# A root chain in two parts, and the four sums of y shared anew between VectorE and GpSimd

## The chip, the cores and the metric

The kernel runs on one core of a Trainium2 chip. A core has a matmul engine (TensorE, PE in the profile; its weight loads are PEld), VectorE (DVE), ScalarE (ACT), GpSimd (POOL) and SyncE (SP), each with its own instruction queue that runs in order, and 16 DMA engines. SBUF is the on-chip working memory, PSUM the memory that matmuls write, in eight banks. The metric is the device time in microseconds (us), the median of several runs.

## The reference

Two blocks follow each other on x of shape (8, 4224, 192), all in float32.

```python
# block 1: causal convolution, 7 taps, one softmaxed tap vector per head (8 heads of 24 channels)
w = softmax(weight, axis=-1)
y[b, s, h, g] = sum_k w[h, k] * x_pad[b, s + k, h, g]
# block 2: layer norm without shift, two matmuls, residual
mu, var = mean(y), mean((y - mu) ** 2)            # over the 192 channels
xn = (y - mu) / sqrt(var + 1e-6) * g_ln
out = y + relu(xn @ w_ch1) @ w_ch2                # 192 -> 768 -> 192
```

The mean and g_ln are folded into w_ch1 once, at the start, and the factor 1/sqrt(var + 1e-6), here rstd, is positive, so it passes through the relu: the kernel multiplies the un-normalised y and scales each row of the product with rstd at the end.

## The kernel before

**Tiles.** The rows are cut into 18 groups. Groups 0 to 2 are small (6, 8 and 10 rows on each of 128 partitions); groups 3 to 17 hold 16 rows on each partition. Groups 3 to 17 are the "mixed" ones, and this text is about them.

**Two stages per group.** `up_mixed(g)` makes the hidden layer (line L521 of the profile), `down_fast(g)` the second matmul (L789). Both use a Winograd form of Strassen's scheme: both operands are cut into four quarters, and seven products of quarters take the place of eight. Each stage so has seven products, 504 matmul instructions for a whole group. What this saves on TensorE is paid in sums on the other engines: sums of y's quarters (`sums_of_y`, L575 to L579), of the weights' quarters (made once), and of the results' quarters (closings and half sums).

**Sums of y.** With quarters a11, a12, a21, a22 of the transposed y, the products need s1 = a21 + a22, s2 = s1 - a11, s3 = a21 - a11 (the sign is taken up in the weights) and s4 = a12 - s2. Before the change GpSimd makes s3 and s2 (L575, L576), and VectorE makes s4 and s1 after the moments (L578, L579). The order of products in the up stage is a11, a12, s2, s3, s1, a22, s4.

**The up stage in two passes.** Pass one is for one third of the hidden columns (PAIR..FC), pass two for the rest. The result's quarters c11, c12, c21, c22 lie in SBUF. ScalarE evicts a product from PSUM (`evict`, L616); a later product that is to be added to a quarter is "closed" (`close`): ScalarE evicts it to a spare place and GpSimd issues a DMA that adds it (`add_by_dma`, L583). In pass one the spare places are parts of pass two's own quarters: c12's for the closings of c11 and c22, c22's for the closing of c21. So ScalarE may not evict into pass two's c22 before the DMA that adds c21 has read its source. In pass two the spare places are two other tiles (parts_cs, parts_tb). In the last group the closings are VectorE's (L622), without DMA.

**The down stage.** Four products, then on VectorE nine half sums over the hidden quarters (L756, three for each of three sums), then three products that need them. Between products ScalarE evicts (L795) and works off a list `work`: a relu of a quarter of the hidden layer (L629), scales of the group before (L869), and the first two taps of the convolution of group g + 2 (L383, L394). The second tap is added to y by two DMAs that GpSimd issues (L397), in order, behind ScalarE's part of them. At the stage's end VectorE takes the moments (L439) of group g + 1 and the sums of its y are made.

**The root.** rstd of two groups is made at once on GpSimd by `root(g)`, after the down stage of each odd group from 3 on (groups 3 and 4 together, 5 and 6, and so on to 15 and 16), and of group 17 alone after that of group 16. It is a chain of 19 small instructions of 128x32 (L457 to L470): seven for the variance and the first guess, then three Newton steps of four. GpSimd's queue before the up stage of an even group is therefore: the two adds of the second tap, s3, s2, the chain, a memset in the input tile of group g + 2 (L160), and then the three closing adds of pass one.

**Order.** No planner reorders anything: each engine runs its instructions in the order in which the program text emits them, and waits on semaphores for what others made. Generators (`yield`, `next`) are used to emit a function's instructions in parts at given places of another.

Of the kernel before, what the change touches and what calls it, by code (L numbers as in the profile page):

```python
# [11 lines left out]
ALU = mybir.AluOpType  # L12
# [4 lines left out]
def kernel(  # L17
# [29 lines left out]
    nc = tc.nc  # L47
# [22 lines left out]
    groups = [(0, 0, 6), (None, 0, LEFT), (0, 6, J - 6), (0, J, J)]  # L70
# [352 lines left out]
    sums = {}  # L423
# [14 lines left out]
        for j in range(j1, n if j2 is None else j2):  # L438
            nc.vector.bn_stats(out=sums[g][:, j, :], in_=y[g][:, j, :])  # L439

    def root(g):
        both = [k for k in (g, g + 1) if k < NG and chain_of(k) == g]
        n = sum(groups[k][2] for k in both)
        st = sums[g]
        dt = spool.tile([P, 2 * J], F32, tag="d", name=f"d{g}")
        vt = spool.tile([P, 2 * J], F32, tag="v", name=f"v{g}")
        rt = spool.tile([P, 2 * J], F32, tag="r", name=f"r{g}")
        d, v, r = dt[:, 0:n], vt[:, 0:n], rt[:, 0:n]

        def affine(dst, src, scale, bias):  # L450
            nc.gpsimd.tensor_scalar(
                out=dst, in0=src, scalar1=scale, scalar2=bias, op0=ALU.mult, op1=ALU.add
            )

        nc.gpsimd.tensor_tensor(d, st[:, 0:n, 1], st[:, 0:n, 4], op=ALU.subtract)  # L457
        nc.gpsimd.tensor_tensor(v, st[:, 0:n, 2], st[:, 0:n, 5], op=ALU.add)
        nc.gpsimd.tensor_tensor(d, d, d, op=ALU.mult)
        affine(v, v, 1.0 / D, 1e-6)  # L460
        affine(d, d, 0.25, 0.0)
        nc.gpsimd.tensor_tensor(v, v, d, op=ALU.add)


        affine(r.bitcast(I32), v.bitcast(I32), -0.5, float(0x5F3759DF))
        for _ in range(3):
            nc.gpsimd.tensor_tensor(d, r, r, op=ALU.mult)  # L467
            nc.gpsimd.tensor_tensor(d, d, v, op=ALU.mult)
            affine(d, d, -0.5, 1.5)
            nc.gpsimd.tensor_tensor(r, r, d, op=ALU.mult)  # L470
        for k in both:
            rstd[k] = rt[:, (k - g) * groups[g][2] :]

    def store_y(g, queue=nc.sync):
        n = groups[g][2]
# [92 lines left out]
    def sums_of_y(g, engine):  # L568

        room = upool.tile([P, 3 * HJ * CH * C], F32, tag="ys", name=f"ysums{g}")  # L570
        room = room.rearrange("p (v j c t) -> p v j c t", v=3, c=CH, t=width(g))
        s2, s3, s4 = [room[:, v] for v in range(3)]
        a11, a12, a21, a22 = quarters_of_y(g)
        ysums[g] = a21, s2, s3, s4
        engine.tensor_tensor(s3, a21, a11, op=ALU.subtract)  # L575
        engine.tensor_tensor(s2, s3, a22, op=ALU.add)  # L576
        yield
        nc.vector.tensor_tensor(s4, a12, s2, op=ALU.subtract)  # L578
        nc.vector.tensor_tensor(a21, a21, a22, op=ALU.add)  # L579
        yield  # L580

    def add_by_dma(dst, src):
        nc.gpsimd.dma_start(out=dst, in_=src, accum_op=ALU.add)  # L583

    def up_mixed(g, ahead):


        W = HJ * C
# [60 lines left out]
        p.evict(X, p.c11)  # L649
        p.product(Y, a12, p.b21)  # L650
        p.close(p.c11, Y, two.c12[:, 0:1])
        p.product(X, s2, p.t[0], False, False)
        p.evict(X, p.c21)
        p.product(Y, s3, p.t[1], True, False)
        p.evict(Y, p.c22)
        p.product(X, s1, p.b12, False, False)
        p.close(p.c22, X, two.c12[:, 1:2])
        p.product(Y, a22, p.t[2], False)
        p.close(p.c21, Y, two.c22[:, 0:1])
        p.product(X, s4, p.b22, False)  # L660
# [28 lines left out]
        p.close(p.c22, Y, rooms[1][:, 0:PAIR])  # L689
        p.product(X, a22, p.t[2], False)  # L690
        p.relu(p.c11)
        lower_sum(g, (PAIR,))
        p.close(p.c21, X)
        p.product(Y, s4, p.b22, False)
# [7 lines left out]
        taps_of_next(5, 6, heads=(H // 2, H))  # L702
        taps_of_next(6, K)

        work = [lambda: one.relu(one.c22)]

        def scale_one(j):
            scale(g - 1, j, j + 1)
            if j == 7:
# [1 line left out]
            elif j == done - 1:  # L711
                add_to_out(g - 1, 8, done)

        if not last:
            work += [lambda j=j: scale_one(j) for j in range(2, done)]
        half = [lambda i=i: two.relu(two.c22[:, i : i + 1]) for i in range(PAIR)]
        return work[0:9] + half + work[9:]

# [53 lines left out]
    def down_fast(g, work):  # L772
        n = fast[g]
        t = width(g)
        w = n * T
        a = of_products(g)
        flat = cpool.tile([P, NC, NFAST * C], F32, tag="cs", name=f"cs{g}")[:, :, 0 : n * C]
        order = "p c (h j t) -> p c h j t" if t == C else "p c (j h t) -> p c h j t"
        cs = flat.rearrange(order, h=2, t=t)
        free = a[:, 1, 0].rearrange("p f q j t -> p (f q) j t")  # L780
        parts = [free[:, 0:CH], free[:, CH : 2 * CH]]
        banks = [take_bank() for c in range(CH) for i in range(2)]

        def product(bank, left, right, to, first, behind=0):
            for c in range(CH):
                dst = banks[2 * c + bank]
                for f in (PAIR, *range(PAIR)):
                    for q in range(NQ):
                        nc.tensor.matmul(  # L789
                            dst[C * q : C * q + C, 0:w], right[:, f, C * c : C * c + C],  # L790
                            left[:, f, q], start=(first and f == PAIR), stop=(f == PAIR - 1),
                            skip_group_check=True,
                        )
                if to is not None:
                    nc.scalar.copy(  # L795
                        to[:, c], dst[:, 0:w].rearrange("p (j t) -> p j t", t=t)
                    )
                for one in work[:behind]:
                    one()
                del work[:behind]  # L800

        b = quarters_of_w2()
        c11, c21 = cs[:, 0:CH, 0], cs[:, 0:CH, 1]
        c12, c22 = cs[:, CH:NC, 0], cs[:, CH:NC, 1]
        if g + 2 < NG:
            work += [
                lambda tap=tap, h=h: tap(g + 2, heads=(h, h + 1))
                for tap in (first_tap, second_tap) for h in range(H)
            ]
        product(0, a[:, 0, 0], b[0], c11, True, 3)  # L810
        product(1, a[:, 1, 0], w2sums[:, 2], c22, True, 2)
        product(1, a[:, 1, 1], w2sums[:, 3], c21, False, 2)
        product(1, a[:, 0, 1], b[2], None, True, 3)
        if g + 1 < NG:
            transpose(g + 1)
        half_sum(g, (1, 1), (1, 1), (1, 0), ALU.add)
        half_sum(g, (0, 0), (1, 1), (0, 0), ALU.add)
        half_sum(g, (0, 1), (0, 1), (1, 1), ALU.subtract)
        for c in range(CH):
            nc.vector.tensor_tensor(  # L820
                c11[:, c], c11[:, c], banks[2 * c + 1][:, 0:w].rearrange("p (j t) -> p j t", t=t),
                op=ALU.add,
            )
        product(0, a[:, 1, 1], w2sums[:, 1], parts[0], False, 2)
        product(0, a[:, 0, 0], w2sums[:, 0], parts[1], False, 2)
        for one in work:
            one()
        product(0, a[:, 0, 1], b[3], c12, False)
        if g + 1 < NG:
            moments(g + 1)  # L830
            sums = sums_of_y(g + 1, nc.gpsimd)
            next(sums)
            next(sums)
        else:
            finish_fast(g, 0, flat, cs, parts)
        return flat, cs, parts
# [92 lines left out]
    split_words(*words_2)  # L929
    join_words(w2flat, *words_2)  # L930
    store_y(0)
    results = None

    def ahead(g):

# [6 lines left out]
    for g in range(NG):  # L942
        mixed, last = g in MIXED, g + 1 == NG
        if g + 2 < NG:
            load_x(g + 2)
        if mixed:
            work = up_mixed(g, ahead(g))
        else:
            up(g)
        if not fast[g]:  # L950

            conv(g + 1)
            transpose(g + 1)
            if g < 2:
                store_y(g + 1)
                moments(g)
            first_tap(g + 2)
            if g == 2:

                second_tap(g + 2)  # L960
                store_y(g + 1, nc.gpsimd)
            down(g)
            park(g)
            if g == 1:
                finish(0)
                root(0)
                sums_of_quarters([w2sums[:, v] for v in range(4)], *quarters_of_w2())
                moments(2)
                root(2)
                finish(1)  # L970
            elif g == 2:
                b11, b12, b21, b22 = quarters_of_w1()
                sums_of_quarters([b12] + [w1sums[:, v] for v in range(3)], b11, b12, b21, b22)
                later = sums_of_y(3, nc.vector)
                next(later)
                next(later)
                finish(2)
                moments(3)
            continue
        if g + 2 < NG:  # L980
            store_y(g + 1)
        results = down_fast(g, work)
        if last:
            finish_fast(g, 1, *results)
            add_and_store(g, slice(0, fast[g]))
            down(g)
            finish(g)
        else:
            if g % 2:
                root(g)  # L990
            if g + 2 == NG:
                root(g + 1)


# [28 lines left out]
```

## Time and profile before

| what | value |
|---|---|
| time, median of 3 (lowest to highest) | 979.66 us (979.08 to 981.59) |
| span of the profiled execution | 978.0 us, mean granted TensorE clock 0.996 |
| TensorE, VectorE, ScalarE, GpSimd busy | 955.8, 902.2, 680.8, 261.6 us |
| one half sum, L756 | mean 1.24 us for 135 |
| GpSimd's sums of y, L575 and L576 | 2.50 and 1.95 us on average, 14 each |
| first instruction of the chain, L457, 128x32 | 2.66 us |
| taps of the convolution on VectorE, L408 | 734 instructions, 367 us |
| closing adds room<-room, 512 KB each | 42, median 5.9 us from issue to landing |

The page of a run gives busy times of each engine, then the costliest groups of instructions by line of the program, with what the engine waited for before them. The trace behind it answers for any stretch of time: the order of instructions on each engine, and for each idle time what ended it ("0.86 <-DMA room<-room" means 0.86 us idle until that DMA had landed). A matmul counts as busy until its modelled end, so how long a fixed set of matmuls takes from first start to next stage's first start says more than the busy time. Idle time of an engine off the bound costs nothing.

### The profile page before, as it was taken

The page shows a single profiled execution, that of the slowest core. Times are in us where ns is not written, and L with a number is a line of the kernel's source. Part 1 is how long each engine was busy: PE and PEld are TensorE (multiplying, and loading weights), DVE is VectorE, ACT ScalarE, POOL GpSimd, SP SyncE. Part 2 cuts the span into 40 slices and gives each one's busy share as a digit, 9 for nine tenths or more (in the row PEclk, how much of TensorE's full clock was granted, in tenths as well). Part 3 has the DMA queues.
Part 4 walks back from the last instruction along what each step waited for, and adds up shares of the span by engine and source line. Part 5 has one row for each costly group of instructions (what it writes and reads, how often), then busy time and mean ns, then how long its engine had stood idle before and what let it go on. Part 6 is the DMA issues. An engine that isn't in the chain of part 4 may idle for free.

```text
span 978.0 us, 38335 instructions
## 1 busy us (share of the span) xinstructions
PE 955.8 (98%) x17274; PEld 724.3 (74%) x17274; DVE 902.2 (92%) x1491; ACT 680.8 (70%) x1098; POOL 261.6 (27%) x383
## 2 busy tenths in 40 slices
PE   7999999999999999999999999999999999998997
PEld 6886586676858677786958678786867768695787
DVE  6999999989999999989999899989989899999757
ACT  5625678487787959677796968678695868775351
POOL 2005311612125131512116131532117121342200
PEclk9999999999999999999999999999999999999999
DMA  8343887479787786879687795978777796856031
GB/s 179 116 137 118 174 210 214 105 144 281 143 239 155 212 188 141 231 153 267 137 240 153 185 231 115 269 146 237 160 203 167 145 275 132 192 114 109 2 68 67
DMA packets 26386, 165.15 MB, mean 169 GB/s; under 512 B 3567, under 2 KB 4463, under 8 KB 18542
## 3 DMA queue, kind: packets, MB, share of 16 engines
q0 software_dynamic: 19120, 99.36, 52.0%
q1 hardware_dynamic: 6798, 63.34, 17.6%
q8 instruction: 135, 2.21, 0.9%
q14 instruction: 29, 0.24, 0.1%
q10 hardware_dynamic: 304, 0.00, 0.0%
HBM read 38.95 MB, written 50.33 MB: 91 GB/s over the span
## 4 chain that ended last, share of the span: by engine, by line
PE 72%; DVE 10%; DMA 6%; POOL 5%; ACT 4%; issue 2%; SPq 0%; ACTq 0%; DVEq 0%; POOLq 0%
PE ps L521 36%; PE ps L789 30%; DVE room L756 6%; PE ps L736 6%; DMA room<-room 5%; DVE st L439 2%; POOL d L457 1%; ACT room L616 1%; DMA xg<-in_x_dram 1%; ACT ot L869 1%; ACT room L629 1%; POOL d L467 1%; POOL r L470 1%; POOL room L583 1%; ACT cs L795 1%
## 5 line engine op out<-in xcount | busy, mean ns | idle before, releaser
L408 DVE SCALAR_TENSOR_TENSOR y<-xg,taps,y 128x384 f32<-128x384 f32 (+3 forms) x734 | 367.0, 577 | 1.2 <-ACT y L383 0.6
L789 PE MATMUL ps<-room,w2sums 128*32 128x256 f32 (+1 forms) x4320 | 238.5, 377 | 4.5 <-DVE room L756 3.1
L521 PE MATMUL ps<-yt,w 32*128 32x256 f32 (+2 forms) x4104 | 238.6, 379 | 0.0
L616 ACT COPY room<-ps 128x1024 f32<-128x1024 f32 (+1 forms) x132 | 172.0, 1303 | 83.1 <-PE ps L521 78.5
L521 PEld LDWEIGHTS ps<-yt,w 32*128 32x128 f32 x4104 | 203.6, 185 | 27.5 <-issue 7.0
L789 PEld LDWEIGHTS ps<-room,w2sums 128*32 128x32 f32 x4320 | 142.5, 110 | 95.6 <-DVE room L756 6.7
L789 PE MATMUL ps<-room,w 128*32 128x256 f32 (+1 forms) x3240 | 182.4, 378 | 2.5 <-DVE room L756 2.4
L756 DVE TENSOR_TENSOR room<-room 128x1024 f32<-128x1024 f32 (+1 forms) x135 | 157.8, 1241 | 7.6 <-PE ps L789 7.6
L789 PEld LDWEIGHTS ps<-room,w 128*32 128x32 f32 x3240 | 107.4, 111 | 69.7 <-DVE room L622 5.2
L521 PE MATMUL ps<-ysums,w1sums 32*128 32x256 f32 x2160 | 123.9, 377 | 0.0
L521 PEld LDWEIGHTS ps<-ysums,w1sums 32*128 32x128 f32 x2160 | 110.6, 185 | 9.6 <-issue 1.8
L795 ACT COPY cs<-ps 128x256 f32<-128x256 f32 (+1 forms) x180 | 66.3, 371 | 47.0 <-PE ps L789 47.0
L629 ACT ACTIVATE room<-room 128x1024 f32<-128x1024 f32 (+1 forms) x75 | 90.8, 1235 | 9.9 <-DMA room<-parts_cs 9.5
L869 ACT ACTIVATE ot<-ot,r 128x192 f32<-128x192 f32 x232 | 93.8, 463 | 0.0
L876 POOL DMA_DIRECT2D out_dram<-ot x40 | 34.4, 1091 | 204.5 <-ACT ot L869 126.1
L622 DVE TENSOR_TENSOR room<-room,ps 128x2048 f32<-128x2048 f32 (+1 forms) x20 | 42.5, 2128 | 45.5 <-PE ps L521 45.3
L383 ACT ACTIVATE y<-xg,taps 128x384 f32<-128x384 f32 (+3 forms) x141 | 72.7, 609 | 8.2 <-DVE st L439 6.9
L439 DVE BATCH_NORM_STATS2 st<-y 128x6 f32<-128x192 f32 x264 | 70.1, 341 | 0.0
L795 ACT COPY room<-ps 128x256 f32<-128x256 f32 (+1 forms) x90 | 33.7, 374 | 49.8 <-PE ps L789 46.9
L521 PE MATMUL ps<-yt,w1sums 32*128 32x256 f32 x1080 | 65.0, 379 | 2.8 <-ACT room L616 2.7
L521 PE MATMUL ps<-ysums,w 32*128 32x256 f32 x1080 | 64.8, 378 | 0.0
L394 ACT ACTIVATE tb<-xg,taps 128x384 f32<-128x384 f32 x112 | 62.0, 637 | 0.0
(103 smaller groups left out, 894.9 us busy)
## 6 DMA issues: line engine op xcount, KB each, us to landing
xg<-in_x_dram SPq DMA_DIRECT2D x15, 2112.0 KB, 17.7
out_dram<-ot POOLq DMA_DIRECT2D x29, 768.0 KB, 8.7
y<-tb POOLq DMA_DIRECT2D x28, 768.0 KB, 10.7
room<-room POOLq DMA_DIRECT2D x42, 512.0 KB, 5.9
out_dram<-y SPq DMA_DIRECT2D x13, 1536.0 KB, 9.9
room<-parts_cs POOLq DMA_DIRECT2D x14, 1024.0 KB, 8.5
room<-parts_tb POOLq DMA_DIRECT2D x14, 1024.0 KB, 7.5
xg<-in_x_dram SPq DMA_DIRECT2D x1, 1536.0 KB, 8.0
```

The source lines that it names most:

```text
L383: nc.scalar.mul(y[g][:, 0:n, cs], xg[g][:, 0:n, cs], taps[:, h, 0:1])
L394: nc.scalar.mul(tb[g][:, 0:n, cs], xg[g][:, 1 : 1 + n, cs], taps[:, h, 1:2])
L408: nc.vector.scalar_tensor_tensor(out=y[g][:, 0:n, cs], in0=t[:, k : k + n, cs], scalar=taps[:, h, k : k + 1], in1=y[g][:, 0:n, cs], op0=AL ...
L439: nc.vector.bn_stats(out=sums[g][:, j, :], in_=y[g][:, j, :])
L521: nc.tensor.matmul(banks[:, q, i * w : i * w + w], right[rows, c, P * i : P * i + P], left[rows, :, c, :], start=(first and c == 0 and i = ...
L616: nc.scalar.activation(dst, src, AF.Relu) if relu else nc.scalar.copy(dst, src)
L629: nc.scalar.activation(c, c, AF.Relu)
L736: nc.tensor.matmul(bank[C * q : C * q + C, 0:w], w2[:, f, C * c : C * c + C], left, start=(f == 0), stop=(f == NF - 1),)
L756: nc.vector.tensor_tensor(a[:, *dst, f], a[:, *left, f], a[:, *right, f], op=op)
L789: nc.tensor.matmul(dst[C * q : C * q + C, 0:w], right[:, f, C * c : C * c + C], left[:, f, q], start=(first and f == PAIR), stop=(f == PAI ...
L795: nc.scalar.copy(to[:, c], dst[:, 0:w].rearrange("p (j t) -> p j t", t=t))
L869: nc.scalar.mul(ots[g][:, j, :], ots[g][:, j, :], rstd[g][:, j : j + 1])
```

## The change

There are four edits.

1. `root` becomes a generator of two parts. Part one is the variance, the first guess and the first two multiplications of Newton's first step (nine instructions), part two the other ten. `up_mixed` emits part one behind the closing of c11 in pass one, part two behind the closing of c22, so that the closing adds don't all stand behind the whole chain. The roots of the first groups are emitted whole, as before.
2. `sums_of_y`: VectorE makes s1 and s2 first, ahead of the moments; GpSimd makes s3 and s4. s1, s2 and s3 lie in the tile ysums, s4 takes the place of a21.
3. When GpSimd makes its two, VectorE first writes one element of s3 with a memset. GpSimd's write of s3 must then wait for that memset, which stands behind VectorE's half sums and its own two sums.
4. In the last group the relus of c22 (both passes) are emitted in the up stage ahead of the last lower sums, and no longer from the list `work` in the down stage.

```diff
-    def root(g):
+    def root(g, whole=False):
...
-        for _ in range(3):
+        for k in both:
+            rstd[k] = rt[:, (k - g) * groups[g][2] :]
+        for step in range(3):
             nc.gpsimd.tensor_tensor(d, r, r, op=ALU.mult)
             nc.gpsimd.tensor_tensor(d, d, v, op=ALU.mult)
+            if step == 0 and not whole:
+                yield
             affine(d, d, -0.5, 1.5)
             nc.gpsimd.tensor_tensor(r, r, d, op=ALU.mult)
-        for k in both:
-            rstd[k] = rt[:, (k - g) * groups[g][2] :]
+        yield
...
-        s2, s3, s4 = [room[:, v] for v in range(3)]
+        s1, s2, s3 = [room[:, v] for v in range(3)]
         a11, a12, a21, a22 = quarters_of_y(g)
-        ysums[g] = a21, s2, s3, s4
+        ysums[g] = s1, s2, s3, a21
+        nc.vector.tensor_tensor(s1, a21, a22, op=ALU.add)
+        nc.vector.tensor_tensor(s2, s1, a11, op=ALU.subtract)
+        if engine is not nc.vector:
+
+            nc.vector.memset(s3[:, 0:1, 0:1, 0:1], 0.0)
         engine.tensor_tensor(s3, a21, a11, op=ALU.subtract)
-        engine.tensor_tensor(s2, s3, a22, op=ALU.add)
-        yield
-        nc.vector.tensor_tensor(s4, a12, s2, op=ALU.subtract)
-        nc.vector.tensor_tensor(a21, a21, a22, op=ALU.add)
-        yield
+        engine.tensor_tensor(a21, a12, s2, op=ALU.subtract)
...
         p.close(p.c11, Y, two.c12[:, 0:1])
+        next(pending, None)
         p.product(X, s2, p.t[0], False, False)
...
         p.close(p.c22, X, two.c12[:, 1:2])
+        next(pending, None)
         p.product(Y, a22, p.t[2], False)
         p.close(p.c21, Y, two.c22[:, 0:1])
...
         p.relu(p.c11)
+        if last:
+            one.relu(one.c22)
+            p.relu(p.c22)
         lower_sum(g, (PAIR,))
...
-        work = [lambda: one.relu(one.c22)]
...
-        if not last:
-            work += [lambda j=j: scale_one(j) for j in range(2, done)]
+        if last:
+            return []
+        work = [lambda: one.relu(one.c22)]
+        work += [lambda j=j: scale_one(j) for j in range(2, done)]
...
         if g + 1 < NG:
+            sums_of_y(g + 1, nc.gpsimd)
             moments(g + 1)
-            sums = sums_of_y(g + 1, nc.gpsimd)
-            next(sums)
-            next(sums)
...
-            work = up_mixed(g, ahead(g))
+            work = up_mixed(g, ahead(g), pending)
+            pending = iter(())
...
-            if g % 2:
-                root(g)
-            if g + 2 == NG:
-                root(g + 1)
+            if g % 2 or g + 2 == NG:
+                pending = root(g + 1 - g % 2)
```

More of the change, by code (lines that the diff above doesn't have):

```diff
@@ L571, in sums_of_y, with up_mixed @@
         room = room.rearrange("p (v j c t) -> p v j c t", v=3, c=CH, t=width(g))
-        s2, s3, s4 = [room[:, v] for v in range(3)]
+        s1, s2, s3 = [room[:, v] for v in range(3)]
         a11, a12, a21, a22 = quarters_of_y(g)
-        ysums[g] = a21, s2, s3, s4
-        engine.tensor_tensor(s3, a21, a11, op=ALU.subtract)
-        engine.tensor_tensor(s2, s3, a22, op=ALU.add)
-        yield
-        nc.vector.tensor_tensor(s4, a12, s2, op=ALU.subtract)
-        nc.vector.tensor_tensor(a21, a21, a22, op=ALU.add)
-        yield
+        ysums[g] = s1, s2, s3, a21
[3 more added lines that the diff above has]
+            nc.vector.memset(s3[:, 0:1, 0:1, 0:1], 0.0)
+        engine.tensor_tensor(s3, a21, a11, op=ALU.subtract)
+        engine.tensor_tensor(a21, a12, s2, op=ALU.subtract)
     def add_by_dma(dst, src):
         nc.gpsimd.dma_start(out=dst, in_=src, accum_op=ALU.add)
-    def up_mixed(g, ahead):
+    def up_mixed(g, ahead, pending):
         W = HJ * C
@@ L931 @@
     store_y(0)
-    results = None
+    results, pending = None, iter(())
     def ahead(g):
@@ L965 @@
                 finish(0)
-                root(0)
+                next(root(0, True))
                 sums_of_quarters([w2sums[:, v] for v in range(4)], *quarters_of_w2())
                 moments(2)
-                root(2)
+                next(root(2, True))
                 finish(1)
@@ L973 @@
                 sums_of_quarters([b12] + [w1sums[:, v] for v in range(3)], b11, b12, b21, b22)
-                later = sums_of_y(3, nc.vector)
-                next(later)
-                next(later)
+                sums_of_y(3, nc.vector)
                 finish(2)
```

## The prediction

> **What bounds the kernel now.** First the page's busy times, then the matmuls in order of time, cut into stages.
>
> ```profile
> PE 955.8 (98%) x17274; PEld 724.3 (74%) x17274; DVE 902.2 (92%) x1491; ACT 680.8 (70%) x1098; POOL 261.6 (27%) x383
> ```
>
> TensorE is the bound, so an edit can only earn what TensorE loses against its own best stage. I cut the timeline where its line changes from L521 (up) to L789 (down) and asked for busy time by stretch. Columns: stretch, length, busy time per engine, granted clock, DMA share, GB/s. The down stages of groups 3, 4 and 16:
>
> ```profile
> 150.72:182.45 31.73, 29.32 (x508) 17.39 (x504) 31.70 (x44) 20.86 (x45) 8.67 (x7) 0.95 0.82 221
> 211.19:238.63 27.44, 27.44 (x508) 16.16 (x504) 27.40 (x44) 22.72 (x51) 7.21 (x6) 1.00 0.87 238
> 881.70:914.12 32.42, 29.34 (x509) 16.77 (x505) 32.26 (x45) 15.15 (x36) 8.21 (x5) 0.95 0.41 71
> ```
>
> The same 504 matmuls take 27.44 us in a good stage, 4.29 more in group 3, 4.98 more in group 16. About half is idle, the rest a granted clock of 0.95 after the wait. The timeline of VectorE and GpSimd there, beside the same nine half sums of group 7:
>
> ```profile
> 389.88 10.26 DVE L756 TENSOR_TENSOR room<-room 128x1024 f32<-128x1024 f32 x9
> ...
> 893.88 13.52 DVE L756 TENSOR_TENSOR room<-room 128x1024 f32<-128x1024 f32 x9
> ...
> 894.14 2.63 POOL L575 TENSOR_TENSOR ysums<-yt 128x768 f32<-128x768 f32 x1
> 896.84 2.66 POOL L576 TENSOR_TENSOR ysums<-ysums,yt 128x768 f32<-128x768 f32 x1
> ```
>
> GpSimd's sums of y ran inside the half sums, 3.3 us longer, and the product needing the first ones waited 3.08 us (the waits of PE name DVE room L756). In group 3 both sums also fall inside (13.84 us). Elsewhere GpSimd is held until the half sums are nearly over by the two adds of L397 (398.86 in group 7); group 16 has none, in group 3 they come earlier.
>
> Next the up stages. Groups 8, 14 and 16, behind which a root chain runs, and group 9, which has none:
>
> ```profile
> 405.27:434.00 28.73, 28.24 (x508) 25.25 (x504) 25.60 (x42) 20.27 (x17) 13.53 (x25) 1.00 0.73 146
> 741.36:770.63 29.27, 28.23 (x508) 25.25 (x504) 25.47 (x41) 20.27 (x17) 13.75 (x25) 1.00 0.72 145
> 853.74:881.70 27.96, 27.96 (x509) 25.36 (x505) 25.48 (x41) 20.17 (x17) 13.07 (x24) 1.00 0.64 128
> 461.44:489.40 27.96, 27.96 (x509) 25.36 (x505) 25.56 (x42) 20.27 (x17) 4.36 (x5) 1.00 0.74 148
> ```
>
> All stages without a chain take 27.96. The seven with one (groups 4, 6 to 16 in twos) take 28.74, 28.05, 28.73, 28.94, 28.31, 29.27 and 27.96: 4.28 us too long together. The timeline of group 8 says why:
>
> ```profile
> 416.10 2.42 POOL L583 DMA_DIRECT2D room<-room  x3
> ...
> 426.69 1.87 ACT L616 COPY room<-ps 128x2048 f32<-128x2048 f32 x1 [0.86 <-DMA room<-room]
> ...
> 428.61 2.47 PEld L521 LDWEIGHTS ps<-yt,w1sums 32*128 32x128 f32 x48 [0.89 <-ACT room L616]
> ```
>
> The chain fills GpSimd from 405.39 to 415.16, then a 1.05 us memset; only then do the three closing adds go out, in a burst. The third (c21's) lands 9.3 us after its issue at 417.26; ScalarE may not overwrite its source before, and TensorE stands behind ScalarE.
>
> Last, group 17's down stage:
>
> ```profile
> 945.90 2.95 ACT L629 ACTIVATE room<-room 128x1024 f32<-128x1024 f32 x3
> ...
> 949.51 2.89 PE L789 MATMUL ps<-room,w2sums 128*32 128x176 f32 x72 [0.94 <-ACT cs L795]
> ```
>
> Three relus hold up the evictions that free the banks: 144 matmuls take 6.51 us (945.71 to 952.22), the next 144 only 5.37 (954.91 to 960.28). Loss 1.14 us.
>
> **What the skill says.** The Trainium skill, "SBUF — State Buffer", section "Who interferes with whom": a VectorE instruction with two SBUF inputs and a GpSimd instruction that reads SBUF exclude each other for a whole instruction; one with a single SBUF input contends with nothing. The trace agrees: 13.5 against 10.3 us for L756; but L576 beside the one-input moments L439 takes 1.84 us and the 16 moments keep their 4.25. "GPSIMD Engine Reference", "Performance versus the Vector engine", puts an fp32 add at 1.96 times VectorE's; here 1.84 (L576) against 0.94 (L578), the same. "DMA: Bandwidth & Descriptors", "Anatomy of one DMA", says waits and dispatch happen on the issuing sequencer, so an add queued behind arithmetic on GpSimd leaves late; group 8's adds left 10.8 us into the stage, group 9's first 5.0.
>
> **The change part by part.** Times are those of group 8's boundary.
>
> *Sums of y.* VectorE keeps two sums of this size (0.93 and 0.95) and GpSimd two (1.84 each). New is a one-element memset (59 ns, L216) per boundary, and it gates GpSimd: its sums start behind all half sums, L820 and VectorE's two sums, at about 403.0 in group 8. Neither can meet L756 any more. They run beside the moments (402.9 to 407.2, one input), so I take 1.84 each: end 406.75, just ahead of the two-input L842. Needed: s2 at 408.07, made by VectorE at 402.8; s3 at about 409.4, ready 404.9; s4 at 413.52, ready 406.75. No wait. VectorE's 0.06 us is hidden by its 2.2 to 2.7 us of idle ahead of L622. Gain: groups 3 and 16 fall to 27.44, **4.29 + 4.98 = 9.27 us**. With half sums of 1.14 us, the third, sixth and ninth are ready at 897.3, 900.7, 904.1 in group 16, and products of 3.9 us start at 897.4, 901.3, 905.1.
>
> *The root in two parts.* GpSimd's queue becomes: sums, memset of xg (about 408), c11's add, part one (nine instructions), c22's add, part two (ten), c21's add. Most other groups' first add leaves 4.25 us into the stage, here 409.5, busy 0.88. Part one from 410.4: beside one-input transposes an instruction and its gap cost 0.31 us (411.19 to 413.12), the first waits for L842 until 410.9; end 413.9. Source c22 is ready at 413.43, so its add leaves about 414.0, free 414.9. Part two lies beside the two-input taps L408, where four instructions took 1.98 us (413.12 to 415.1): 10 x 0.5 = 5, end 420.0. c21's add therefore leaves at 420.0, *later* than now (417.26), but alone: lone adds landed in 5.3 and 4.4 us in group 9, so about 425.0. ScalarE gets there at 425.83. Bounds on the landing: 4.2 (shortest of all) to 6.9 us (group 9's third, behind another), that is 424.2 to 426.9; the upper end is today's wait again. I take 5.0: the waits go, 0.1 us per group remains; **3.6 of 4.28 us**. Queued behind part two is only c21's add: pass two's parts_cs add leaves at 422.58 now, with GpSimd idle 4.1 us before it. The scale waiting for rstd is at 422.18 on ScalarE, 2.2 us after part two. Group 17's root is off the path: its closings are VectorE's.
>
> *Relus of the last group.* They move into ScalarE's 4.26 us of idle before 942.86: from 938.6, 1.06 us, then 1.9 us once VectorE's close ends at 939.87: end about 941.8. Gain **1.14 us**.
>
> *Keeping rstd earlier in the text, running the first roots whole, group 3's sums in another order:* the same instructions, nothing.
>
> Sum: 9.27 + 3.6 + 1.14 = 14.0; 979.66 - 14.0 = **965.7 us**.
>
> **Rivals.**
> A. *The root's split earns nothing*: part two ahead of c21's add replaces the burst's delay by its own. For it: the add leaves 2.7 us later and my margin is 0.8 us. Against: it lands alone. Time: 979.66 - 10.4 = 969.3.
> B. *The new order of sums costs a little at each boundary*: GpSimd meets L842, or VectorE finishes later. For it: the end of s4 lies 0.4 us ahead of L842. Against: six microseconds of slack for s4, two on VectorE. At 0.2 us for 14 boundaries: 965.7 + 2.8 = 968.5.
> C. *Slower*: if c21's add still needs 9 us, it lands at 429.0, ScalarE waits 3.2 us instead of 0.86, seven times 2.3 = 16 us instead of a gain: 979.66 - 10.4 + 16 = 985. Against: no first add of a burst took over 5.5 us in group 8, and none is ahead of it.
>
> **How the numbers follow.** Forecast 0.70, A 0.15, B 0.09, C 0.06. The range reaches down to all of 14.7 us plus the 1.2 us by which three down stages behind late chains (groups 6, 12, 14) exceed 27.44: 963.8, and a run's scatter: 963.3. Up: A and a little of C, 971.5. Faster means under 976.7: the first three cases, 0.94; the same 0.01; slower 0.05.
>
> **What would show it.** Right: down stages of groups 3 and 16 near 27.4 with nine half sums in 10.3 us and GpSimd's sums behind them at 1.84; stages with a chain at 28.0 to 28.1, no ScalarE wait on DMA room<-room, single adds landing in about 5; group 17's first 144 w2sums matmuls in 5.4. Wrong: c21's add leaving after 421 or landing after 426; scales waiting for GpSimd; TensorE waiting for s3 or s4.

## The result, and the profile after

The changed kernel takes **964.04 us** (median of 4 runs, 962.95 to 965.15) against 979.39 us for the kernel before, measured beside it (979.08 to 981.59): ratio 0.9839, 95% interval 0.9819 to 0.9858, or 15.4 us less. Forecast were 965.7 us, range 963.3 to 971.5.

The page's first line of busy times, now for a span of 962.8 us:

```profile
PE 950.3 (99%) x17274; PEld 717.0 (74%) x17274; DVE 897.2 (93%) x1505; ACT 680.9 (71%) x1097; POOL 249.4 (26%) x383
```

Busy time by stretch, cut as before where the matmuls change from up to down (columns: stretch, length, busy time of PE, PEld, DVE, ACT, POOL, granted clock, DMA share, GB/s). In this order: the down stages of groups 3, 4 and 16, the up stages of groups 8, 14, 16 and 9, the down stage of group 17:

```profile
150.61:178.05 27.44, 27.44 (x509) 16.12 (x505) 27.30 (x39) 20.84 (x45) 5.46 (x6) 1.00 0.87 239
206.00:233.45 27.45, 27.45 (x508) 16.12 (x504) 27.27 (x39) 22.71 (x51) 5.42 (x6) 1.00 0.87 237
872.52:899.97 27.45, 27.45 (x509) 16.10 (x505) 27.28 (x39) 15.04 (x35) 3.66 (x4) 1.00 0.48 84
399.66:427.72 28.06, 28.06 (x509) 25.52 (x505) 25.82 (x47) 20.27 (x17) 14.47 (x26) 1.00 0.74 150
733.75:761.71 27.96, 27.96 (x509) 25.31 (x505) 25.80 (x47) 20.26 (x17) 14.47 (x26) 1.00 0.74 149
844.56:872.52 27.96, 27.96 (x509) 25.32 (x505) 25.80 (x47) 20.21 (x17) 13.48 (x25) 1.00 0.64 128
455.17:483.12 27.95, 27.95 (x508) 25.31 (x504) 25.81 (x47) 20.26 (x17) 6.06 (x6) 1.00 0.74 149
928.88:947.79 18.91, 18.91 (x505) 16.33 (x509) 12.35 (x19) 7.78 (x21) 0.00 (x0) 1.00 0.06 13
```

The outliers are gone: groups 3 and 16 now have group 4's down stage, also in granted clock, and groups with a chain have group 9's up stage, but for 0.10 us in group 8 that stays unexplained. Adding up the profiled runs' stages gives the whole difference of 15.2 us in the spans:

| stages | before | after | difference |
|---|---|---|---|
| down, groups 3 and 16 | 31.73 + 32.42 | 27.44 + 27.45 | -9.26 |
| up, seven groups with a chain | 200.00 | 195.82 | -4.18 |
| down, group 17 | 20.05 | 18.91 | -1.14 |
| up, group 17 | 28.80 | 28.91 | +0.11 |
| down of groups 6, 11 to 14 | 139.42 | 138.79 | -0.63 |
| all else (the start, rounding) | | | -0.1 |

The row of groups 6 and 11 to 14 isn't the change's alone: nearly every trace has one to four stalls of 0.3 to 1.3 us in down stages of groups 6 to 15, mostly of groups 10 to 12, which differ from trace to trace. The largest is in group 11 before and in group 12 after. Part of group 12's 1.2 us can be read: ScalarE's relu of c11 had waited 1.80 us for the DMA room<-parts_cs just ahead of the stage, and the weight loads then waited for ScalarE. Another 0.48 us of their idle time has no cause that the profile shows.

The waits of the matmuls themselves (longest first: who waited, for whom, us in total, times, longest) are the start's and nothing else. Before, VectorE's half sums stood on top (first line, of the kernel before; then the three of the changed kernel):

```profile
PE ps L789 <- DVE room L756: 5.5, 2, 3.1
```

```profile
PE ps L362 <- POOL room L292: 4.9, 1, 4.9
PE ps L320 <- DMA xg<-in_x_dram: 1.2, 1, 1.2
PE ps L329 <- DVE room L245: 0.8, 1, 0.8
```

The timeline of group 16's boundary on VectorE and GpSimd (half sums are L765 now, GpSimd's sums L583 and L584):

```profile
884.66 10.26 DVE L765 TENSOR_TENSOR room<-room 128x1024 f32<-128x1024 f32 x9
...
897.73 0.06 DVE L582 MEMSET ysums<- 128x1 f32 x1
...
897.96 1.84 POOL L583 TENSOR_TENSOR ysums<-yt 128x768 f32<-128x768 f32 x1 [12.72 <-DVE ysums L582]
899.88 1.82 POOL L584 TENSOR_TENSOR yt<-yt,ysums 128x768 f32<-128x768 f32 x1
```

GpSimd idles 12.7 us for the gate and loses nothing by it: its two sums then take 1.84 and 1.82 us beside the moments, where they took 2.63 and 2.66, and the nine half sums take 10.26 us in place of 13.52.

The timeline of group 8's up stage, which starts at 399.66 (closing adds are L587, evictions L620):

```profile
403.91 0.88 POOL L587 DMA_DIRECT2D room<-room  x1 [1.52 <-ACT room L620]
...
408.09 0.89 POOL L587 DMA_DIRECT2D room<-room  x1
...
414.39 0.88 POOL L587 DMA_DIRECT2D room<-room  x1
...
420.21 1.86 ACT L620 COPY room<-ps 128x2048 f32<-128x2048 f32 x1
```

The three adds leave one by one, 4.25, 8.43 and 14.73 us into the stage. The last landed 4.4 us later, at +19.2, and ScalarE's eviction, which waited 0.86 us for it before, starts at 20.55 without a wait.

### The profile page after: what moved, and what is told of

Same layout as the page of the kernel before. It is cut to its first block, busy times and chain, and to the rows that moved or that the text cites. A ratio compares the mean times of both kernels' runs of the same rounds, so it can differ in the third digit from the quotient of the medians.

```text
span 962.8 us, 38387 instructions
## 1 busy us (share of the span) xinstructions
PE 950.3 (99%) x17274; PEld 717.0 (74%) x17274; DVE 897.2 (93%) x1505; ACT 680.9 (71%) x1097; POOL 249.4 (26%) x383
## 4 chain that ended last, share of the span: by engine, by line
PE 96%; DMA 2%; DVE 2%; issue 0%; DVEq 0%
PE ps L524 48%; PE ps L798 41%; PE ps L745 6%; DMA xg<-in_x_dram 1%; DVE room L765 1%; PE ps L320 1%; DVE room L626 0%; DMA ga<-in_moe_g_ln_dram 0%; PE ps L344 0%; PE ps L349 0%; DVE y L890 0%; PE ps L332 0%; DVE room L774 0%; DVE ot L915 0%; DVE ot L900 0%
## 5 line engine op out<-in xcount | busy, mean ns | idle before, releaser
L524 PE MATMUL ps<-yt,w 32*128 32x256 f32 (+2 forms) x4104 | 235.6, 379 | 0.1
L620 ACT COPY room<-ps 128x1024 f32<-128x1024 f32 (+1 forms) x132 | 172.0, 1303 | 78.7 <-PE ps L524 78.6
L798 PEld LDWEIGHTS ps<-room,w2sums 128*32 128x32 f32 x4320 | 137.8, 110 | 93.4 <-ACT room L633 5.5
L765 DVE TENSOR_TENSOR room<-room 128x1024 f32<-128x1024 f32 (+1 forms) x135 | 151.0, 1190 | 6.4 <-PE ps L798 6.4
L798 PEld LDWEIGHTS ps<-room,w 128*32 128x32 f32 x3240 | 103.9, 110 | 69.1 <-DVE room L626 5.2
L626 DVE TENSOR_TENSOR room<-room,ps 128x2048 f32<-128x2048 f32 (+1 forms) x20 | 42.5, 2127 | 34.9 <-PE ps L524 34.7
```

Source lines behind the costliest of these rows:

```text
L524: nc.tensor.matmul(banks[:, q, i * w : i * w + w], right[rows, c, P * i : P * i + P], left[rows, :, c, :], start=(first and c == 0 and i = ...
L620: nc.scalar.activation(dst, src, AF.Relu) if relu else nc.scalar.copy(dst, src)
L765: nc.vector.tensor_tensor(a[:, *dst, f], a[:, *left, f], a[:, *right, f], op=op)
L798: nc.tensor.matmul(dst[C * q : C * q + C, 0:w], right[:, f, C * c : C * c + C], left[:, f, q], start=(first and f == PAIR), stop=(f == PAI ...
```

## The experiments

They ran on three chips, on which the kernel before takes 984.0 to 984.4 us; in the traces taken there the start, up to the first product of group 0, is 2 to 4 us longer. So times are given as ratios to the kernel before on the same chip, and the stages of the traces carry the argument. Gate alone, no gate, split alone and relus alone ran on one of the three. The changed kernel itself was run once more on each of the other two, as the measure for the others:

> The changed kernel itself, so that the others have it on the same chip. Both theories: every up stage but the last 28.0 us, every down stage near 27.4 us; about 964 us where the kernel before has 979, and a few us more on a chip where the first groups are slower.

> The changed kernel again, as the measure for the three others on this chip: the same stages as before, 0.984 of the kernel before.

Measured: 0.9835 (0.981 to 0.9859) and 0.9829 (0.9813 to 0.9845), 967.72 and 967.21 us. All stages are as in the first profile (27.96 and 27.45 us), but for stray stalls.

**The gate alone.** The kernel before, with GpSimd's sums held back (the moments stand later in the text only so that VectorE writes the one element ahead of them):

```diff
         ysums[g] = a21, s2, s3, s4
+        if engine is not nc.vector:
+            nc.vector.memset(s3[:, 0:1, 0:1, 0:1], 0.0)
         engine.tensor_tensor(s3, a21, a11, op=ALU.subtract)
...
-            moments(g + 1)
             sums = sums_of_y(g + 1, nc.gpsimd)
             next(sums)
+            moments(g + 1)
             next(sums)
```

> The kernel before with the one-element memset alone: VectorE writes it behind its half sums, GpSimd still makes s3 and s2, VectorE s4 and s1 behind the moments. Theory (the gate alone frees the half sums): the down stages of groups 3 and 16 fall from 31.73 and 32.42 us to 27.4, nine half sums take 10.3 us everywhere, the up stages behind a chain stay too long; gain 9.3 us, about 970.1 us. Rival (the new shares of the four sums matter): less than 6 us, or a new wait of TensorE for s4 or s1, which VectorE makes last.

Measured: 0.9914 (0.9891 to 0.9937), 8.5 us less. The down stages of groups 3 and 16 are 27.43 and 27.44 us. On this chip they are 30.04 and 32.15 without the gate (from the relu experiment below, which leaves them alone), so the gate is worth 7.3 us here. The up stages behind a chain stay too long, by 6.7 us together. Of the 2.0 us that are missing from the forecast, 1.7 are TensorE's clock in group 3: in the trace of the kernel before, the granted clock falls to 0.50 for 3.41 us near the end of that down stage, and in the trace of the relu experiment it doesn't. The columns are stretch, length, busy time of PE, granted clock, DMA share, GB/s; first the kernel before, in the slow stretch and in as long a time behind it, then the relu experiment, in the whole down stage:

```profile
177.90:181.31 3.41, 3.41 (x40) 0.50 0.69 141
181.31:184.72 3.41, 3.41 (x65) 1.00 0.03 7
```

```profile
152.98:183.02 30.04, 27.66 (x509) 1.00 0.86 233
```

The slow stretch costs half of 3.41 us, 1.70, and 31.73 less 1.70 is 30.03. Group 16 has such a stretch in both traces. The timeline of group 16 in this kernel:

```profile
896.21 10.26 DVE L758 TENSOR_TENSOR room<-room 128x1024 f32<-128x1024 f32 x9
...
907.64 1.84 POOL L577 TENSOR_TENSOR ysums<-yt 128x768 f32<-128x768 f32 x1 [10.76 <-DVE ysums L576]
909.57 1.84 POOL L578 TENSOR_TENSOR ysums<-ysums,yt 128x768 f32<-128x768 f32 x1
```

So the half sums need only the gate, whoever makes which sum.

**No gate.** The changed kernel without its memset:

```diff
-        if engine is not nc.vector:
-            nc.vector.memset(s3[:, 0:1, 0:1, 0:1], 0.0)
```

> The changed kernel without the memset: GpSimd may start s3 as soon as y is transposed, s4 still waits for VectorE's s2. Theory (a two-input sum on GpSimd holds up a two-input sum on VectorE for its whole length): s3 meets one half sum in groups 3 and 16, which then takes 2.8 us in place of 1.2; TensorE loses about 2 us in group 16 and 1 in group 3, some 3 us against the changed kernel, about 967 us. Rival (the sharing of the sums, not the gate, made the gain): as the changed kernel, 964.0 us.

Measured: 0.9857 (0.9833 to 0.9882); the interval overlaps with the changed kernel's, which were taken on other chips, so the stages decide. Down stages of groups 3 and 16: 28.43 and 29.09 us, 1.0 and 1.65 over 27.44, as expected; all other groups are as in the changed kernel, but for stray stalls. Group 16:

```profile
887.99 11.91 DVE L762 TENSOR_TENSOR room<-room 128x1024 f32<-128x1024 f32 x9
...
888.26 2.60 POOL L580 TENSOR_TENSOR ysums<-yt 128x768 f32<-128x768 f32 x1
```

One two-input sum on GpSimd makes the nine half sums 1.65 us longer (11.91 against 10.26); two of them made it 3.26 in the kernel before.

**A write in the sum's place.** As the last one, but GpSimd only writes s3:

```diff
-        engine.tensor_tensor(s3, a21, a11, op=ALU.subtract)
+        if engine is nc.vector:
+            engine.tensor_tensor(s3, a21, a11, op=ALU.subtract)
+        else:
+            engine.memset(s3, 0.0)
```

> The changed kernel without the gate, and GpSimd's s3 replaced by a memset of the whole of s3 to zero (so s3's products are left out of the result); the memset reads nothing and may run beside the half sums in groups 3 and 16, as the ungated s3 did. Theory (only a GpSimd instruction that reads SBUF holds up VectorE's two-input sums): nine half sums take 10.3 us in both groups, their down stages 27.4 to 27.5 us. Rival (any GpSimd work on SBUF beside them costs the same): one half sum of 2.5 us or more in each, down stages of 28.4 and 29.1 us as with the ungated s3.

Measured: 0.9836 (0.9819 to 0.9852), down stages of groups 3 and 16 at 27.44 and 27.45 us. The timeline of group 16:

```profile
887.47 10.27 DVE L765 TENSOR_TENSOR room<-room 128x1024 f32<-128x1024 f32 x9
...
887.72 1.06 POOL L583 MEMSET ysums<- 128x768 f32 x1
```

The memset runs inside the half sums for 1.06 us and costs them nothing. It is GpSimd's reading of SBUF that excludes VectorE's two-input sums, as the Trainium skill says in "SBUF — State Buffer", section "Who interferes with whom"; that GpSimd is at work is not enough.

**All four sums on VectorE.** GpSimd then makes none, and no gate is written.

```diff
-            sums_of_y(g + 1, nc.gpsimd)
+            sums_of_y(g + 1, nc.vector)
```

> The changed kernel with all four sums of y on VectorE, so that GpSimd has none, ahead of the moments. VectorE gets 1.9 us more work in each of 14 groups, GpSimd loses 3.65. VectorE idles about 2.0 us ahead of its second-pass closing L626 now. Theory (that idle hides it): stages as in the changed kernel within 0.2 us each, time the same within 0.3%. Rival (VectorE is a second bound, and the share given to GpSimd is part of the gain): 0.5 us or more in each of 14 groups, 7 us or more slower, with TensorE waiting for L626.

Measured: 0.9838 (0.9822 to 0.9854) against 0.9829 (0.9813 to 0.9845) for the changed kernel on the same chip: no difference that these runs can tell. Up stages are 27.88 us, even 0.08 shorter, but for groups 6, 16 and 17 (28.12, 28.23, 29.52). The last two miss the expected 0.2 us: group 16 is 0.27 us longer than in the changed kernel and group 17 is 0.60. Elsewhere VectorE's idle ahead of its closing L626 paid, as the waits of VectorE show, first of the changed kernel, then of this one:

```profile
DVE room L626 <- PE ps L524: 35.7, 17, 3.1
```

```profile
DVE room L626 <- PE ps L524: 9.7, 6, 3.1
```

VectorE's busy time grows from 897.4 to 921.7 us, 96% of the span, and TensorE hardly notices. That GpSimd has a share in the sums is no part of the gain that these times can tell; that its share doesn't meet the half sums is.

**The split alone.** The kernel before with `root` in two parts, emitted behind the closings of c11 and c22 (the change's lines for `root`, `pending` and the two `next(pending, None)`, no others).

> The kernel before with the root in two parts alone. Theory (the burst of closing adds behind the chain costs 4.3 us over seven stages): every up stage behind a chain falls to 28.0 us, c21's add leaves about 14.7 us into the stage and lands in about 5; the down stages of groups 3 and 16 stay at 31.7 and 32.4; gain 4.3 us, about 975.1 us. Rival (the split helps only with the sums' new order, since s3 and s2 run later or earlier): gain under 2 us.

Measured: 0.9909 (0.9884 to 0.9934), 9.0 us less, twice what was expected. The up stages give 7.7 of it. Groups 4 to 16 in twos:

| kernel | 4 | 6 | 8 | 10 | 12 | 14 | 16 | over 7 x 27.96 |
|---|---|---|---|---|---|---|---|---|
| before, chip of the result | 28.74 | 28.05 | 28.73 | 28.94 | 28.31 | 29.27 | 27.96 | 4.3 |
| relus alone, this chip | 31.84 | 29.80 | 28.05 | 28.66 | 28.49 | 29.28 | 27.96 | 8.4 |
| split alone, this chip | 28.44 | 28.17 | 27.96 | 27.96 | 27.96 | 27.96 | 27.96 | 0.7 |

The relu experiment runs the up stages of these groups as the kernel before. Its 8.4 us exceed the 4.3 through groups 4 and 6, with 3.1 and 1.7 us more. In group 6 the add of c21 was issued at nearly the same time (12.3 against 12.1 us into the stage) and landed 1.8 us later, at 22.39 instead of 20.60. In group 4 the burst left 1.7 us later and landed 1.4 us later, at 22.74, and behind the wait the granted clock fell to 0.50 for 3.41 us, which costs another 1.70 us (columns as above; the slow stretch and the time behind it):

```profile
208.87:212.28 3.41, 3.41 (x40) 0.50 0.37 77
212.28:215.69 3.41, 3.41 (x64) 1.00 0.98 202
```

So the waits come to 6.7 us here and to 4.3 in the first trace. Whether the chip makes this difference or the single execution isn't shown, since each has one trace. The clock has a part in the time too: its mean is 0.994 over the 27 runs of the kernel before on this chip and 0.997 over the six of the split. As an estimate, 0.003 of 980 us is some 3 us of the 9.0; which of the waits brings the lower clock isn't shown. What is left of it with the split is 0.48 us in group 4, where c21's add landed at 21.03; the 0.2 us of group 6, whose add landed in time (19.91), have another cause, which stays open.

**The last group's relus alone.**

```diff
         p.relu(p.c11)
+        if last:
+            one.relu(one.c22)
+            p.relu(p.c22)
...
+        if last:
+            return []
```

> The kernel before with the last group's relus of c22 moved into its up stage alone. Theory: the first 144 matmuls with w2sums of group 17 fall from 6.51 to 5.37 us, nothing else changes; gain 1.1 us, about 978.3 us. Rival (ScalarE's earlier relus delay the eviction of c12 or the closing): no gain, 979.4 us.

Measured: 0.9991 (0.998 to 1.0002). The down stage of group 17 falls from 20.05 to 18.90 us, its up stage stays at 28.80: 1.15 us, less than the time can show. The three parts alone add up to 18.3 us on this chip, more than the 16.2 and 16.8 of the whole change on the other two; with intervals of over 2 us either way for gate and split, that is no contradiction.

**The chain in one piece, everything else changed.**

```diff
-                pending = root(g + 1 - g % 2)
+                next(root(g + 1 - g % 2, True))
```

> The changed kernel with the root chain in one piece at its old place, ahead of the three closing adds; sums, gate and relus as changed. Theory (the adds wait behind the chain, and the chain now starts 1.6 us later, behind GpSimd's s3 and s4): the burst leaves about 12.2 us into the stage in place of 10.9, c21 lands past 22 us, and each stage behind a chain loses 1.5 to 2 us; 10 to 17 us more than the changed kernel. Rival (the parts add up): 4.3 us more, as the split's share of the prediction, or the 8 us that the split alone earned on the last chip.

Measured: 0.9923 (0.9898 to 0.9947), 8.5 us over the changed kernel on the same chip, the rival's number; the up stages lose 9.6 us together, 0.5 to 1.9 each. My theory was half wrong: the burst left at 11.3 us in most of these groups, not at 12.2. The chain does start later, but VectorE's s4 and s1 no longer stand in its way: its first instruction takes 0.92 us in place of 2.66.

**Part two behind c21.** In the changed kernel, the second `next(pending, None)` moved behind the closing of c21.

> The changed kernel with the root's second part behind the closing of c21 in place of that of c22. c21's add then leaves about 10 us into the stage in place of 14.7, part two ends at about 16, the first scale that reads rstd stands at 17.0. Theory (since 14.7 is early enough, nothing waits any more): the same time as the changed kernel within 0.3%. Rival (c21's add is still late in some stages, as its landing varies): up to 3 us faster. Other rival (rstd comes too late for ScalarE): slower by 7 times some tenths of a us, with ScalarE waiting on GpSimd.

Measured: 0.9836 (0.9812 to 0.986), the changed kernel's time. c21's add left at 9.86 us and landed at 16.0 to 16.9; no ScalarE wait on GpSimd appears. The margin to 20.55 us grows from between 0 and 1.6 us (a landing at 18.9 to 20.55 in the changed kernel on this chip) to about four and buys nothing, since TensorE didn't wait.

**c21's add 3 us later.**

```diff
             nc.gpsimd.tensor_tensor(r, r, d, op=ALU.mult)
+        for _ in range(0 if whole else 6):
+            affine(d, d, 1.0, 0.0)
         yield
```

> The changed kernel with six more instructions of 128x32 on GpSimd at the end of the root's second part, on a tile that is dead by then, so that c21's add leaves 3 us later, about 17.7 us into the stage. Theory (ScalarE needs c21's source at 20.5 us, and a lone add lands in 4.4 to 5.5 us): c21 lands at 22 to 23 us, ScalarE waits 1.6 to 2.5 us, TensorE loses 1.4 to 2.2 us in each of seven stages; 10 to 15 us slower than the changed kernel. Rival (DMA time is hidden, the gain of the split came from the chain's own contention with VectorE): the same time.

Measured: 1.0002 (0.9987 to 1.0017), 16.3 us over the changed kernel: the whole gain of the change undone by 3 us of GpSimd. Lines of the timeline of group 8 (adds L589, evictions L622), then the waits:

```profile
421.47 3.06 POOL L451 TENSOR_SCALAR d<-d 128x32 f32<-128x32 f32 x6
...
424.57 0.88 POOL L589 DMA_DIRECT2D room<-room  x1
...
429.28 1.87 ACT L622 COPY room<-ps 128x2048 f32<-128x2048 f32 x1 [2.01 <-DMA room<-room]
```

```profile
ACT room L622 <- DMA room<-room: 14.1, 7, 3.2
ACT room L635 <- DMA room<-parts_cs: 12.7, 9, 2.5
PE ps L526 <- ACT room L622: 11.5, 7, 2.8
```

The seven up stages lose 13.8 us together, and 2.9 us more falls on the down stages behind three of them (groups 4, 12 and 14), where the next add, now queued behind the late one, lands late too.

Set beside each other, the runs give one rule for this wait. When c21's add lands, in us from the stage's start, and how much longer than 27.96 us the stage is:

| kernel, group | lands at | loss |
|---|---|---|
| changed, 6 | 20.55 | 0.00 |
| before, 12 | 20.90 | 0.35 |
| before, 8 | 21.32 | 0.77 |
| before, 14 | 21.87 | 1.31 |
| chain in one piece, 6 | 22.12 | 1.57 |
| six more instructions, 4 | 22.33 | 1.78 |
| six more instructions, 10 | 23.67 | 3.12 |

The loss is the landing less 20.55 us: TensorE pays every microsecond past the time at which ScalarE wants the place, and nothing before it. Of 169 up stages (groups 4 to 16 in the traces of all kernels but the one with all sums on VectorE) 163 follow this within 0.06 us. Five are 0.1 to 0.2 us longer than it says, and one, group 4 of the relu experiment, is 1.7 us longer (3.88 us for a landing at 22.74): that is the slow stretch of the clock shown above.

**One step further.** The changed kernel with part two behind c21, and the last group's pass-one closings by ScalarE and DMA as in the other groups:

```diff
-                if part is None or last:
+                if part is None or (last and self.n == PAIR):
```

> The changed kernel with two edits: part two of the root behind the closing of c21 (as tried before, same time), and in the last group the three closings of pass one by ScalarE and DMA as in all other groups, in place of VectorE's sum from PSUM. Theory (in the last group TensorE waits for VectorE's closings, L626): its up stage falls from 28.91 to about 28.2 us, 0.7 us faster, which the time hardly tells but the stage does. Rival (the adds land too late for the last group's relus): the stage grows, or the down stage behind it waits for ScalarE.

Measured: 0.9827 (0.9811 to 0.9842), 966.74 us, against 0.9829 and 967.21 us for the changed kernel on the same chip. The up stage of group 17 falls from 28.92 to 28.49 us, 0.43 of the expected 0.7, and the down stage stays at 18.90. The stage is better; the time can't tell.

## Why the prediction was right

**Sums of y.** Right in mechanism and size: 9.27 us forecast, 9.26 in the stages. That they agree to 0.01 us is luck in part. Of the 9.27, 3.4 us are the two slow stretches of the clock in the trace that the forecast was read from. In the changed kernel they are gone with the waits. But group 3 was traced twice more with its waits (relus alone, split alone) and took 30.04 us both times, at full clock; from those traces the forecast would have been 7.3 to 7.5. The forecast times of group 8's boundary also held: GpSimd's sums ran 1.83 and 1.82 us (1.84 forecast), the last ended about 1.75 us into the stage (1.5 forecast), TensorE waited for none. The experiments add that gate and shares are separate things, and that only the gate pays. The prediction left out one limit: the Trainium skill, "SBUF — State Buffer", section "Who interferes with whom", says of VectorE instructions with at most one SBUF input that they don't contend with GpSimd, but only outside VectorE's 2-port modes. What the argument needs is measured: GpSimd's sums took 1.84 and 1.82 us beside the moments.

**The root in two parts.** c21's add was forecast to leave at 420.0 in the time of the run before, 14.73 us into the stage; it left at 14.73. I took 5.0 us for its landing, with bounds 4.2 and 6.9; measured in seven groups 4.4 to 6.0. So rival A's reason was real, the add does leave later than before, but it lands alone. The margin was thin: in group 6 it landed at 20.55, the very limit, and in a later trace (no gate) at 20.72, which cost 0.17 us. The term was a little small, 3.6 us against 4.18, since I left 0.1 us per group for a rest that isn't there. In the experiments it came to more: 9.0 us for the split alone, where the stages that it mends had 6.7 us of waits and 1.7 us from the clock, and 8.5 for the chain in one piece, where c21's add also left 0.2 to 1.3 us later than in the kernel before. The forecast took seven landings of a burst from one trace. It could not see that c21's landing moves by up to 1.8 us from trace to trace, and that every such microsecond past 20.55 is paid.

**Rival C** was right about what would happen if the add were late, and 3 us of delay brought it about; the condition did not occur.

**Rival B** failed because VectorE has idle time: it could take 1.9 us more in each group (all four sums on VectorE), where B feared 0.2. In group 17 alone B has something: its up stage is 28.91 or 28.92 us in the traces with the new shares, gate or not, and 28.80 in those with the old shares, gate or not (the two experiments that change this stage further left aside).

**Relus.** 1.14 us forecast and measured.

**The rest** of the difference, 0.6 us, is the stray stalls of the down stages. No experiment was made for them; the traces show a late DMA ahead of some, and no cause for the others.

## What to carry to other kernels

An in-order queue that issues DMAs shouldn't hold arithmetic ahead of them that nobody needs soon: find for each DMA the time by which its landing is wanted, and place long chains in the gaps, so that the transfers leave singly. When the bound engine waits for a second engine's instructions that are sometimes longer than usual, look at what a third engine runs at that moment, and if it has time, hold it back with a wait on a cheap instruction; or, if the second engine has idle time elsewhere, give it the work (all four sums on VectorE took the same time). A part that a run's time can't tell is still to be seen in the length of its stage.

## What the runs showed of the hardware

- Three DMA adds of 512 KB issued within 1.2 us landed 4.3 to 5.5, 6.1 to 8.1 and 8.5 to 9.8 us after issue in the kernel before (group 14: 4.25, 6.18, 9.64), the third up to 10.5 in the run of the gate alone; c21's add without the two others beside it landed in 4.4 to 6.0 in the changed kernel.
- A GpSimd instruction of 128x32 beside VectorE's two-input taps took 0.41 to 0.50 us, the first one behind the issue of an add 0.81 (at 408.75 in the changed kernel); beside VectorE's one-input transposes such instructions took 0.21 to 0.26. The 28 taps took 14.90 us with and without a chain beside them (groups 8 and 9).
- A GpSimd memset of 128x768 ran in 1.06 us inside VectorE's two-input half sums of group 16 and cost them nothing, where a two-input sum of the same size cost them 1.65 us.
- The granted clock fell to 0.50 for 3.41 us in the middle of three of the fourteen traces: before (groups 3 and 16), split alone (group 16) and relus alone (groups 4 and 16). Each time TensorE had waited in that stage, and each time 1.70 us were lost; other waits as long, such as 2.8 us in the run with c21's add 3 us later, were followed by no such stretch. When it comes isn't shown.
